# A fused attention and feed-forward kernel: the order of all pieces written out as one sequence in place of a list scheduler

## The chip, the cores and the metric

The kernel runs on one core of one Trainium2 chip. The metric is the device time of one execution in microseconds (us). Five engines work side by side, each through its own list of instructions in order: TensorE (PE, with its weight loads shown as PEld), VectorE (DVE), ScalarE (ACT), GpSimd (POOL) and SyncE (SP). POOL issues the loads; SP, and at the end ACT, issue transposing transfers and stores.

## The reference

Nyström attention over 8 batches, 8 heads, 576 rows of 64, with 32 landmark rows per head (means of 18 rows), and a feed-forward layer behind it. Everything is float32 in DRAM.

```python
q_lm = q.reshape(B, H, m, S // m, D).mean(axis=3)      # m = 32
k_lm = k.reshape(B, H, m, S // m, D).mean(axis=3)
A  = softmax(scale * q @ k_lm.T)                       # 576 x 32
Bm = softmax(scale * q_lm @ k_lm.T)                    # 32 x 32
C  = softmax(scale * q_lm @ k.T)                       # 32 x 576
Z = Bm.T / (norm_1(Bm) * norm_inf(Bm) + 1e-06)
for _ in range(6):
    Z = 2 * Z - Z @ Bm @ Z
x = (A @ Z @ C @ v)           # then heads side by side: 4608 x 512
h = x @ w_in                  # 512 x 2048
out = (h * sigmoid(h)) @ w_out # 2048 x 512
```

## The kernel before, in words

One pass over the 8 batches. The kernel first describes its work as 1,473 named pieces (`Op`, line 38), each with the engine or engines that may run it, the instructions that it emits, the pieces that it depends on, a priority, and the PSUM banks that it opens and releases. `Plan.run` (line 84) then puts all pieces into one order and gives each a PSUM bank, and the loop at line 1164 emits them in that order. What an engine executes is its own part of that order.

The pieces, by the names that the texts use (`.b` is the batch, `@5b00` and `@5b20` are the two row groups of batch b in layer 2, `@5340` and `@5740` a third group shared by four batches):

- `ld1`, `ld0` (lines 447, 453): loads of k (1) and q (0), for batch 0 in two halves each. `ldv0` to `ldv2` (460): three parts of v. `wi..` (467, 471): three loads for each quarter of `w_in`. `wo0` to `wo3` (477): quarters of `w_out`. All on POOL; at most eight are under way.
- `const` and `ident` (487 to 499): constants; `zer` feeds the filler products.
- `tr`, `trc` (568, 406/404): transposes of q and k on PE and copies out, for batches 0 to 2. From batch 3 on `xt10, xt11, xt00, xt01` (592), transposing transfers on SP, in their place. `ct0`, `ct1` (856) are the same for the exponentials of C from batch 2 on (`ctm`, `ctc` on PE and DVE or ACT before).
- `lms`, `lmc` (394, 404): landmark sums on PE for batches 0 and 1; `lra` to `lrd` (628): the same by additions on DVE from batch 2 on. `ltr`, `lmT`: their transposes.
- `sb`, `pb`, `pbs`, `pbr`, `bmx`, `bmt`, `csb`, `bbd`, `n1`, `nrm`: Bm with its softmax and norm; `pb` is an Exp on ACT.
- `f0`, `stz`, `stf`, and six times `ns` (PE) and `nsd` (DVE, line 754): the Newton iteration for Z. Each step waits for the one before.
- `A`, `Ax`, `S`, `Ln`, `Rs`, `etn`: the softmax of A; `C`, `Cx`, `wrc`: that of C. `A` and `C` open four banks at once and are 16 small products on parts of PE ("packed"). `Ax`, `Ln`, `Rs` and `Cx` are ACT's.
- `cv`, `wc`, `zbd`, `zt`, `ztc`: C @ v and Z times it. `m0` to `m3` and copies `mc` (404 on ACT, 406 on DVE): that times a quarter of `w_in`, so that layer 1 is `etn` times `m`.
- `h0` to `h15` and `hx0`, `hx8` (PE, 394): layer 1; `g..` and `gx..` (ACT, 956 and 979): Silu on the way out of PSUM. Silu and Exp/Ln are in different ACT tables, and each change between them is a table load.
- `o0` to `o3`, `oc`: layer 2 of the first group, plain. All other groups are done as pairs (`layer2_pair`, line 1025) with seven products `p1` to `p7` in place of eight, sums `ss` and `wt` on DVE beforehand, and `c..`, `u2` as evacuations into an output tile `ost` (a ring of six). `os..` stores it.

`Plan.run` of before is a list scheduler. It keeps a clock of its own, durations from simple formulas (lines 302 to 311), a lag after each piece, and a margin of 0.4 us in front of most PE pieces. Whenever an engine is idle in that clock it takes the ready piece of lowest priority number, to which the table `ORDER` (line 19) adds a correction for some fifty pieces. Other rules: no Silu between the Exp/Ln pieces of a batch, and PSUM pools: layer 2 gets banks 7, 6 and 5, layer 1 at most four of banks 4 to 0 (one, while a batch of Exp/Ln is pending), the rest the lowest free of 0 to 5 or 6. An evacuation that may run on ACT or DVE (`either`, line 413) goes to whichever is idle. While PE has nothing ready in the first 45 us of that clock, it gets a filler (`warm`, line 495): a product of zeros of 256 columns into bank 7.

Two waits are part of the description and not of the order: a transposing transfer of batch b waits for the second v load of batch b (line 594, `gate`), and the loads of batch b for the third transfer `xt00` of batch b-1 and for `ct0` of batch b-2 (line 1141).

Of the kernel before, what the change touches and what calls it, by code (L numbers as in the profile page):

```python
# [18 lines left out]
ORDER = {  # L19
    "f0.0": (200.69, 0), "A.0": (-135.46, 12.93), "Ln11.0": (-57.289, 0), "etn1.0": (-31.554, 0),  # L20
    "ctm00.0": (-1364.2, 0), "wc.0": (-5319.5, 0), "mc11.0": (-629.91, 0), "tr10.1": (-42.668, 0),
    "trc15.1": (-1007.6, 0), "tr19.1": (-457.92, 0), "tr114.1": (-85.703, 0),
    "tr00.1": (-4845.1, 0), "tr09.1": (-1.1208, 0), "tr014.1": (-139.96, 0),
    "lms116.1": (413.98, 0), "lms000.1": (-607.71, 0), "lms006.1": (-83.37, 0),
    "lms010.1": (328.48, 0), "nsd00.1": (-627.38, 0), "ns10.1": (2306.7, 0),
    "nsd10.1": (-1204.8, 0), "A.1": (-266.77, 0), "Ax10.1": (-230.29, 0), "Rs1.1": (-127.11, 0),
    "Cx00.1": (-281, 0), "Cx01.1": (-181.38, 0), "Cx11.1": (-2693.4, 0), "tr014.2": (-314.54, 0),
    "bbd.2": (-120.57, 0), "nsd40.2": (175.02, 0), "h15.1": (234.98, 0), "lrd1.3": (-791.6, 0),
    "A.3": (-480.16, 0), "S00.3": (52.867, 0), "Ln01.3": (24.258, 0), "Ax11.3": (-2.2697, 0),
    "h3.2": (185.78, 0), "hx0.2": (41.862, 0), "h11.2": (452.76, 0), "hx8.2": (-6.3754, 0),  # L30
    "p5@5200.0": (-179, 0), "c12@5220.0": (-251.23, 0), "A.4": (-78.982, 0),
    "etn1.4": (1667.8, 0), "Cx11.4": (29.753, 0), "cv0.4": (-3300.5, 0),
    "p6@5340.0": (-4.9303, 0), "p7@5340.0": (-4146.8, 0), "Ax10.6": (162.02, 0),
    "ss00@5500.0": (-5226.2, 0), "p7@5700.0": (633.04, 0), "p4@5720.0": (524.17, 0),
}
# [31 lines left out]
class Plan:  # L67
# [3 lines left out]
    WARM = 45.0  # L71
# [9 lines left out]
    start_warm = 1.1  # L81
    filler = None

    def run(self):
        import heapq
        order = []
        for o in self.ops:
            o.left = len(o.deps)
            shift, o.ready = ORDER.get(o.name, (0.0, 0.0))
            o.prio += shift  # L90
            for d in {id(d): d for d, _ in o.deps}.values():
                d.users.append(o)
        cand = {e: [] for e in self.LAG}
        idle = {"PE": 1.0, "ACT": 1.0, "DVE": 0.9, "POOL": 1.3, "SP": 1.0}
        banks = [0] * 8
        table = ["exp"]
        group = [None, 0]
        pending = [False]
        groups = {}
        for o in self.ops:  # L100
            if o.group is not None:
                groups[o.group] = groups.get(o.group, 0) + 1
        tiled = [None]
        dmaq = [0.0]
        events = sorted(set(idle.values()) | {o.ready for o in self.ops})
        waiting = []

        def activate(o):
            for e, _ in o.engs:
                cand[e].append(o)  # L110

        for o in self.ops:
            if not o.left:
                activate(o)

        l1_at = set()
        l1_open = {}
        l1_seen = set()
        l2_on = [False]
        l2_open = {}  # L120
        wide = [False]

        def fit(o):
            if o.cls == "L2":
                pool = (7, 6) if wide[0] else (7, 6, 5)
                if o.pair is not None and l2_open:
                    n = sum(not banks[i] for i in pool)
                    if o.pair != next(iter(l2_open)) and (o.pair in l2_open or n < 2):
                        return None
            elif o.cls == "L1":  # L130
                room = 1 if pending[0] or group[0] is not None and group[1] > 3 else 4
                if wide[0]:
                    return None
                if len(l1_at) >= room:
                    return None
                pool = (4, 3, 2, 1, 0)
            else:
                pool = (0, 1, 2, 3, 4, 5) if l2_on[0] else (0, 1, 2, 3, 4, 5, 6)
            free = [i for i in pool if not banks[i]]
            return tuple(free[:o.psum]) if len(free) >= o.psum else None  # L140

        n = 0
        total = len(self.ops)
        while n < total:
            if not events:
                raise RuntimeError("plan stuck: " + ", ".join(
                    f"{o.name}" for e in cand for o in cand[e])[:600])
            t = heapq.heappop(events)
            while events and events[0] <= t + 1e-9:
                heapq.heappop(events)  # L150
            moved = True
            while moved:
                moved = False
                for e in ("PE", "ACT", "DVE", "POOL", "SP"):
                    if idle[e] > t + 1e-9:
                        continue
                    best, bslot, later, soon = None, None, None, None
                    if e == "PE":
                        wide[0] = any(o.psum == 4 and o.ready <= t + 1e-9 and (
                            o.opens is None or group[0] == o.opens) for o in cand[e])  # L160
                    for o in cand[e]:
                        r = o.ready + o.margin
                        if r > t + 1e-9:
                            if later is None or r < later:
                                later = r
                            if o.crit and (soon is None or r < soon):
                                soon = r
                            continue
                        rank = o.prio
                        if e == "PE" and tiled[0] and o.tiled == tiled[0]:  # L170
                            rank -= 1e5
                        if best is not None and rank >= brank:
                            continue
                        if e == "ACT" and o.table == "silu" and group[0] is not None:
                            continue
                        if e == "ACT" and o.group is not None and group[0] != o.group:
                            if o.early is not None and table[0] == "exp":
                                pass
                            elif group[0] is not None or l1_open:
                                continue  # L180
                            elif o.early is not None and any(
                                    x.done is None or x.done > t + 1e-9 for x in o.early):
                                continue
                            elif len(l1_at) > 2:
                                pending[0] = True
                                continue
                        if o.opens is not None and group[0] != o.opens and (
                                group[0] is not None or l1_open or len(l1_at) > 2):
                            if group[0] is None and not l1_open:
                                pending[0] = True  # L190
                            continue
                        s = None
                        if o.psum:
                            s = fit(o)
                            if s is None:
                                continue
                        best, bslot, brank = o, s, rank
                    if best is None:
                        if later is not None:
                            heapq.heappush(events, later)  # L200
                        if e == "PE" and not banks[7] and self.start_warm <= t < self.WARM and (
                                later is None or later > t + 0.12):
                            end = t + (0.22 if t < self.start_warm + 4.4 else 0.11)
                            order.append((self.filler, e, t, end, False))
                            idle[e] = end
                            heapq.heappush(events, end)
                            tiled[0] = None
                        continue
                    o = best
                    if soon is not None and not o.crit:  # L210
                        d = max(d2 for e2, d2 in o.engs if e2 == e)
                        if t + d > soon + 0.06:
# [3 lines left out]
                    for e2, d2 in o.engs:  # L216
                        cand[e2].remove(o)
                        if e2 == e:
                            dur = d2
# [95 lines left out]
def kernel(  # L315
# [95 lines left out]
    A = P.add  # L411
# [794 lines left out]
```

## Time and profile before

| | us |
|---|---|
| median of three runs | 249.36 |
| the three runs | 247.73, 249.66, 249.36 |
| span of the profiled execution, first to last instruction | 246.7 |
| PE busy in it | 238.9 |
| ACT busy in it | 183.6 |
| DVE busy in it | 171.8 |
| share of the chain that ended last that is PE's | 83% |

The span of the profiled execution lies 1.0 to 3.0 us below the three runs' own times; the page gives no other time of that execution. In the lines of groups: source line, engine, operation, tile written and tiles read, count, busy time and mean duration of one in ns, then the idle time before them and what ended it. In a timeline: start, length (from the first start to the last end of a merged row), engine, line, operation, tiles and count. A matmul's record covers its way through the array, so that records of back-to-back matmuls overlap; the distance between starts is what each costs PE.

### The profile page before, as it was taken

Reading aid. Unit: us, or ns where it says so; the run is one execution under the profiler, and the core shown is the slowest. Engines: PE = TensorE matmul, PEld = TensorE weight load, DVE = VectorE, ACT = ScalarE, POOL = GpSimd, SP = SyncE. Lnnn points to the kernel's source line nnn. Section 1 sums busy time; section 2 is a strip of 40 time slices with the busy share of each in tenths; the row PEclk is TensorE's granted clock in tenths of the full one; section 3 lists DMA queues with packets and bytes.
Section 4 is the critical chain, followed back from the end, with each engine's and each line's share of the span. In section 5 each row is a group of like instructions: output and inputs, shape, how many; then the busy total and the mean of one; then the engine's idle time right before and its main releaser. Section 6 shows DMA issues by size and latency. Waiting matters only on the chain.

```text
span 246.7 us, 7075 instructions
## 1 busy us (share of the span) xinstructions
PE 238.9 (97%) x2771; PEld 170.8 (69%) x2771; DVE 171.8 (70%) x441; ACT 183.6 (74%) x438; POOL 37.2 (15%) x63
## 2 busy tenths in 40 slices
PE   8999999999979999999999999999999999999993
PEld 6786565566767645577886655697886566688883
DVE  2368956495869956949999879189798667066632
ACT  2597996599865999998668998966988978822200
POOL 8435733200022003200220040000000000000000
PEclk9999999999999999999999999999999999999999
DMA  5999999999999979989899799897443003022352
GB/s 103 203 203 193 196 208 206 207 246 166 181 115 215 208 145 152 212 135 158 168 233 229 150 170 226 146 184 99 118 119 101 0 3 85 3 73 62 82 141 72
DMA packets 55874, 36.50 MB, mean 148 GB/s; under 512 B 36641, under 2 KB 47393, under 8 KB 55841
## 3 DMA queue, kind: packets, MB, share of 16 engines
q0 software_dynamic: 15264, 18.35, 44.6%
q1 hardware_dynamic: 39808, 16.92, 33.2%
q10 hardware_dynamic: 768, 0.79, 1.3%
q8 instruction: 21, 0.34, 0.5%
q14 instruction: 13, 0.10, 0.1%
HBM read 36.70 MB, written 9.44 MB: 187 GB/s over the span
## 4 chain that ended last, share of the span: by engine, by line
PE 83%; DMA 7%; DVE 3%; ACT 3%; SPq 1%; issue 1%; POOL 0%; DVEq 0%; POOLq 0%
PE ps L394 80%; DMA qT<-qk 4%; DMA qk<-in_q_dram 3%; PE ps L568 2%; SPq L592 1%; ACT m L404 1%; DVE red L628 1%; PE ps L844 1%; DVE st L754 1%; ACT ce L829 1%; ACT L956 1%; POOL qk L447 0%; ACT ln L794 0%; DVE etn L803 0%; DVE ss L1044 0%
## 5 line engine op out<-in xcount | busy, mean ns | idle before, releaser
L394 PE MATMUL ps<-etn,m 128*128 128x512 bf16 (+1 forms) x512 | 68.9, 286 | 0.4 <-ACT gm L956 0.4
L956 ACT ACTIVATE gm<-ps 128x512 f16<-128x512 f32 x128 | 66.1, 652 | 2.0 <-PE ps L394 1.8
L394 PEld LDWEIGHTS <-gm 128*128 128x128 f16 x512 | 48.7, 98 | 11.3 <-issue 2.4
L394 PE MATMUL ps<-w_out_sb,gm 128*128 128x256 f16 (+1 forms) x392 | 53.6, 281 | 0.0
L394 PEld LDWEIGHTS <-m 128*128 128x128 bf16 x512 | 32.0, 98 | 24.0 <-issue 1.8
L404 ACT COPY ost<-ps 128x256 f32<-128x256 f32 (+1 forms) x48 | 18.4, 383 | 37.4 <-PE ps L394 30.3
L394 PEld LDWEIGHTS <-ss 128*128 128x128 f16 x408 | 39.1, 98 | 6.6 <-issue 0.9
L1079 DVE TENSOR_TENSOR ost<-ost,ps 128x256 f32<-128x256 f32 x51 | 21.2, 416 | 20.4 <-PE ps L394 14.2
L394 PE MATMUL ps<-wt,ss 128*128 128x256 f16 x272 | 34.1, 273 | 0.0
L754 DVE SCALAR_TENSOR_TENSOR st<-st,ps 128x320 bf16<-128x320 bf16 (+3 forms) x54 | 21.4, 404 | 9.0 <-PE ps L394 7.8
L406 DVE CAST m<-ps 128x512 bf16<-128x512 f32 x31 | 20.0, 683 | 0.4 <-PE ps L394 0.2
L406 DVE COPY ost<-ps 128x256 f32<-128x256 f32 x22 | 9.3, 422 | 14.9 <-PE ps L394 14.8
L404 ACT CAST m<-ps 128x512 bf16<-128x512 f32 x33 | 17.9, 601 | 1.8 <-PE ps L394 1.7
L394 PE MATMUL ps<-w_out_sb,ss 128*128 128x256 f16 x136 | 17.6, 273 | 0.0
L453 POOL DMA_DIRECT2D qk<-in_k_dram x7 | 5.0, 714 | 82.7 <-DMA ct<-ce 41.9
L460 POOL DMA_DIRECT2D v<-in_v_dram x24 | 14.0, 591 | 14.5 <-PE ps L394 6.9
L394 PE MATMUL ps<-zer 128*128 128x256 bf16 x79 | 14.7, 310 | 1.1 <-DVE zer L487 1.1
L394 PE MATMUL ps<-wt,gm 128*128 128x256 f16 x120 | 15.5, 272 | 0.0
L394 PEld LDWEIGHTS <-st 128*128 128x128 bf16 x96 | 8.4, 97 | 9.0 <-issue 2.9
L394 PE MATMUL ps<-st 128*128 128x160 bf16 (+1 forms) x96 | 14.4, 225 | 0.2 <-DVE wsb L889 0.2
L829 ACT ACTIVATE ce<-ps 128x288 bf16<-128x288 f32 x32 | 12.8, 413 | 0.0
L784 ACT ACTIVATE et<-ps 128x288 bf16<-128x288 f32 x32 | 10.6, 423 | 2.3 <-PE ps L394 2.2
(91 smaller groups left out, 331.3 us busy)
## 6 DMA issues: line engine op xcount, KB each, us to landing
out_dram<-ost SPq DMA_DIRECT2D x128, 64.0 KB, 2.1
v<-in_v_dram POOLq DMA_DIRECT2D x24, 192.0 KB, 11.2
qk<-in_k_dram POOLq DMA_DIRECT2D x7, 576.0 KB, 7.5
qk<-in_q_dram POOLq DMA_DIRECT2D x7, 576.0 KB, 10.6
w_out_sb<-in_moe_w_out_dram POOLq DMA_DIRECT2D x4, 512.0 KB, 10.4
w_in_sb<-in_moe_w_in_dram POOLq DMA_DIRECT2D x4, 256.0 KB, 9.2
w_in_sb<-in_moe_w_in_dram POOLq DMA_DIRECT2D x8, 128.0 KB, 7.9
qk<-in_k_dram POOLq DMA_DIRECT2D x2, 288.0 KB, 4.3
```

Source lines behind the costliest of these rows:

```text
L394: nc.tensor.matmul(out=out_ap, lhsT=lhsT, rhs=rhs, start=start, stop=stop, skip_group_check=True)
L404: nc.scalar.copy(out=out, in_=in_)
L406: nc.vector.tensor_copy(out=out, in_=in_)
L453: lambda e, t=t, src=src: nc.gpsimd.dma_start(out=qk_r[b % 2][:, t].rearrange("p g j d -> p g (j d)"), in_=src[b].rearrange("(g h) (l j) d ...
L460: lambda e, a=a: nc.gpsimd.dma_start(out=v_r[b % 2][a * L:(a + 1) * L, :, :], in_=v[b].rearrange("h (l a x) d -> a l h (x d)", l=L, a=VA)[ ...
L568: nc.tensor.transpose(out=ps[:, n * 128:(n + 1) * 128], in_=qk[:, t, g, 2 * jp:2 * jp + 2, :].rearrange("p j d -> p (j d)"), identity=idb)
L592: lambda e, t=t, g=g: nc.sync.dma_start_transpose(out=qT[:, t, g], in_=qk[:, t, g].rearrange("p j d -> p (j d)")),
L754: nc.vector.scalar_tensor_tensor(out=s2[:, g0:g1, lo:SW], in0=s[:, g0:g1, lo:SW], scalar=2.0, in1=ps[:, 0:NG * SW].rearrange("p (g x) -> p ...
L784: lambda e, g=g, et=et, c=c: nc.scalar.activation(out=et[:, c], in_=bank(me["A"], 2 * g + c)[:, 0:HS], func=AF.Exp, scale=sc / J),
L829: nc.scalar.activation(out=ce[:, :, 0:VP].rearrange("p (i c) (a l) -> p c a i l", c=2, a=VA)[:, c], in_=bank(me["C"], 2 * g + c)[:, 0:HS]. ...
L956: lambda e, dc=dc, cell=cell: nc.scalar.activation(out=gm[:, dc, :], in_=bank(cell["o"]), func=AF.Silu),
L1079: nc.vector.tensor_tensor(out=out_, in0=x, in1=y, op=OP.add)
```

## The change

`ORDER` and the scheduler go. In their place stands `SEQUENCE`, a text that names every piece once, in the order of emission, with the engine behind a slash where a piece may run on two, and `*n` for n fillers. `Plan.run` walks through it, checks that a piece comes after those that it depends on, and deals PSUM banks from one list: a piece takes the bank at its head, and a bank goes to its tail when the last piece that reads it has been placed in the sequence. Banks 0 to 6 are in the list from the start, bank 7 joins with the first piece of layer 2 (until then fillers write to it). The pools, the limit on layer 1's banks, the margin and the rule on Silu are gone with the scheduler.

PE's list has 53 fillers in place of 79: 22 instead of 20 ahead of the first load, and 31 instead of 59 later. All other products are the same. 77 evacuations change their engine (39 from ACT to DVE, 38 from DVE to ACT). ACT's table loads stay 12, its first included. Line numbers of pieces are 74 lower in the changed kernel, since the scheduler was longer than the sequence.

In `layer1` the product `hx` also names the copies of the first quarter that it reads among its dependencies.

The diff, cut to the new `run`, the parts of the sequence that the texts speak of, and `hx`:

```diff
-ORDER = {
-    "f0.0": (200.69, 0), "A.0": (-135.46, 12.93), "Ln11.0": (-57.289, 0), "etn1.0": (-31.554, 0),
...
-}
+SEQUENCE = """
+ld00.0 const ident *22 tr00.0 lms000.0 lms006.0 lms0012.0 ld01.0 *5 lms010.0 lms016.0 lms0112.0
+tr09.0 tr014.0 trc014.0/DVE tr05.0 trc05.0/ACT trc00.0/ACT ld10.0 *1 lms100.0 lms106.0 tr15.0
+trc15.0/ACT lmc0.0/DVE ltr0.0 lmT0.0/DVE trc09.0/DVE ld11.0 lms1012.0 *4 lms110.0 lms116.0
+lms1112.0 lmc1.0/ACT tr114.0 trc114.0/DVE tr10.0 trc10.0/ACT *1 ltr1.0 lmT1.0/DVE tr19.0
+trc19.0/DVE *3 A.0 Ax10.0 sb.0 pb.0 pbs.0 pbr.0 bmx.0 Ax00.0 Ax11.0 Ax01.0 *4 C.0 Cx00.0 Cx11.0
+Cx01.0 Cx10.0 bmt.0 S10.0 Ln10.0 *2 csb.0 n1.0 bbd.0 ld1.1 lms100.1 lms106.1 *2 f0.0 tr19.1
...
+ltr0.1 lmT0.1/ACT tr00.1 trc00.1/DVE trc15.1/ACT ctm00.0 ns30.0 nsd30.0 ctc00.0/DVE sb.1 pb.1 *1
+C.1 Cx11.1 Cx10.1 Cx00.1 pbs.1 pbr.1 bmx.1 Cx01.1 ns41.0 ns40.0 nsd40.0 nsd41.0 wi0a ldv0.0 ldv2.0
+ldv1.0 cv0.0 cv1.0 wc.0 ns50.0 nsd50.0 csb.1 *2 ns51.0 nsd51.0 n1.1 zbd.0 bmt.1 bbd.1 nrm.1 *3 A.1
+Ax11.1 zt.0 ztc.0/DVE Ax00.1 Ax10.1 Ax01.1 ctm00.1 S11.1 Ln11.1 f0.1 stz.1 stf0.1 ctc00.1/DVE
+wi0b1 wi1a wi0b0 m0.0 mc01.0/ACT mc00.0/ACT *2 ns00.1 S01.1 Ln01.1 nsd00.1 wi2b1 wi1b0 wi1b1 m1.0
+mc11.0/DVE mc10.0/DVE S10.1 Ln10.1 S00.1 Ln00.1 Rs1.1 ctm10.1 ns10.1 nsd10.1 h2.0 ctc10.1/DVE *1
+h7.0 wi2a wi2b0 m2.0 mc20.0/DVE mc21.0/DVE Rs0.1 g2.0 h4.0 ns20.1 nsd20.1 g7.0 h6.0 h0.0 g0.0 h5.0
+g6.0 wi3a wi3b0 wi3b1 m3.0 mc30.0/DVE mc31.0/DVE h10.0 g10.0 h1.0 g1.0 ns30.1 h9.0 nsd30.1 h3.0
...
+etn1.1 wo0 h15.0 o0@5001.0 h11.0 g11.0 ldv1.1 ldv0.1 ldv2.1 cv0.1 wrc.1 fold wc.1 g4.0 o0@5000.0
+zbd.1 g5.0 g15.0 zt.1 ztc.1/ACT h13.0 g13.0 wo1 o1@5001.0 etn0.1 m3.1 mc30.1/DVE m2.1 mc31.1/ACT
+mc21.1/ACT mc20.1/DVE m0.1 mc00.1/ACT mc01.1/DVE o1@5000.0 ld1.2 tr15.2 tr19.2 trc19.2/DVE
...
+trc05.2/ACT o2@5000.0 wo3 o3@5000.0 oc@5000.0/ACT g13.1 o3@5001.0 oc@5001.0/ACT lrb1.2 lrc1.2
...
+ss30@5100.0 sb.2 hx0.1 gx0.1 pb.2 pbs.2 ld1.3 ldv1.3 xt11.3 xt10.3 lra1.3 pbr.2 p5@5020.0
+c5@5020.0/ACT p6@5020.0 u2@5020.0/ACT p1@5100.0 c1@5100.0/ACT l1done.0 C.2 Cx10.2 Cx01.2 Cx00.2
+Cx11.2 ld0.3 xt00.3 p3@5020.0 c12@5020.0 bmx.2 lrb1.3 bmt.2 ss00@5120.0 lrc1.3 p6@5100.0
+u2@5100.0/ACT A.2 Ax11.2 Ax10.2 l1done.1 p7@5020.0 c22@5020.0 Ax00.2 Ax01.2 S11.2 Ln11.2 csb.2
+n1.2 S10.2 Ln10.2 p5@5100.0 c5@5100.0/ACT lrd1.3 ltr1.3 S01.2 lmT1.3/ACT bbd.2 S00.2 f0.2 Ln00.2
+Ln01.2 Rs1.2 Rs0.2 p4@5020.0 p7@5100.0 c21@5020.0/ACT xt01.3 lra0.3 nrm.2 lrb0.3 lrc0.3 stz.2
+lrd0.3 ltr0.3 stf0.2 etn1.2 c22@5100.0 p3@5100.0 etn0.2 lmT0.3/ACT sb.3 pb.3 ns00.2 nsd00.2
+p4@5100.0 c21@5100.0/ACT pbs.3 c12@5100.0 ns10.2 nsd10.2 ct0.2 ct1.2 A.3 Ax11.3 Ax00.3 Ax10.3
+Ax01.3 ss10@5120.0 ldv0.2 ldv1.2 ldv2.2 cv0.2 wrc.2 wc.2 C.3 Cx10.3 Cx00.3 ns20.2 pbr.3 p1@5120.0
...
+g9.2 g4.2 nsd30.3 ns40.3 nsd40.3 ldv1.4 ct0.3 ld0.4 ld1.4 ldv0.3 ct1.3 ldv2.3 cv0.3 xt00.4 ld1.5
...
+os11@5741.0/ACT os13@5741.0/ACT os12@5741.0/SP p3@5740.0 c12@5740.0 os13@5740.0/ACT os11@5740.0/SP
+os10@5740.0/SP os12@5740.0/ACT p4@5740.0 c21@5740.0/DVE os03@5741.0/ACT os00@5741.0/SP
+os01@5741.0/ACT l1done.6 l1done.7 os02@5741.0/SP
+"""
...
     def run(self):
...
+        named = {o.name: o for o in self.ops}
+        free = list(range(7))
+        table = "exp"
         order = []
...
+        seen = set()
+        for word in SEQUENCE.split():
+            if word[0] == "*":
+                order += [(self.filler, "PE", 0.0, 0.0, False)] * int(word[1:])
+                continue
+            name, _, e = word.partition("/")
+            o = named.pop(name)
+            assert all(id(d) in seen for d, _ in o.deps), name
+            seen.add(id(o))
+            if o.psum:
+                if o.cls == "L2" and 7 not in seen:
+                    seen.add(7)
+                    free.append(7)
+                assert len(free) >= o.psum, name
+                o.slot = tuple(free[:o.psum])
+                del free[:o.psum]
+            e = e or o.engs[0][0]
+            switch = e == "ACT" and o.table is not None and o.table != table
+            if switch:
+                table = o.table
+            order.append((o, e, 0.0, 0.0, switch))
+            for p, i in o.frees:
+                p.readers[i] -= 1
+                if not p.readers[i]:
+                    free.append(p.slot[i])
+        assert not named, sorted(named)
         return order
...
                 o = cell["o"] = A(f"hx{d0}.{b}", [("PE", mm_us(64, 16))], xm,
-                                  etn_ops[b] + m_ops[b, dc // 4]
+                                  etn_ops[b] + m_ops[b, d0 // 4] + m_ops[b, dc // 4]
                                   + l2_last.get(("x", b // 4 - 1), []), p + 0.5, psum=1, cls="L1")
```

## The prediction

> **What bounds the kernel now.** I read the page first: busy shares, slices, chain.
>
> ```profile
> span 246.7 us, 7075 instructions
> PE 238.9 (97%) x2771; PEld 170.8 (69%) x2771; DVE 171.8 (70%) x441; ACT 183.6 (74%) x438; POOL 37.2 (15%) x63
> ...
> PE   8999999999979999999999999999999999999993
> ...
> PEclk9999999999999999999999999999999999999999
> DMA  5999999999999979989899799897443003022352
> ...
> PE 83%; DMA 7%; DVE 3%; ACT 3%; SPq 1%; issue 1%; POOL 0%; DVEq 0%; POOLq 0%
> ```
>
> TensorE (PE) is busy from end to end and carries 83% of the chain; ACT and DVE have 63 and 75 us to spare. But busy PE hides two things: matmul records overlap, and fillers (the products of `zer`) count as busy. So I took the groups by shape, then the PE timeline at a few places.
>
> ```profile
> L394 PE MATMUL ps<-zer 128*128 128x256 bf16 x79 | 14.7, 310 | 1.1 <-DVE zer L487 1.1
> ```
>
> ```profile
> 1.12 4.43 PE L394 MATMUL ps<-zer 128*128 128x256 bf16 x20 [1.12 <-DVE zer L487]
> ...
> 12.33 0.20 PE L394 MATMUL ps<-lmT 64*32 64x32 bf16 x4
> ```
>
> ```profile
> 51.34 1.89 PE L394 MATMUL ps<-etn,m 128*128 128x512 bf16 x8
> ```
>
> ```profile
> 72.74 0.27 PE L394 MATMUL ps<-rs,fold 128*128 128x256 f16 x1 [1.63 <-DVE st L754]
> ```
>
> ```profile
> 88.64 0.59 PE L394 MATMUL ps<-etn,m 128*128 128x512 bf16 x2 [0.39 <-ACT gm L956]
> ...
> 96.43 0.62 PE L394 MATMUL ps<-w_in_sb,zt 64*32 64x512 bf16 x16
> ```
>
> ```profile
> 241.93 1.04 PE L394 MATMUL ps<-wt,gx 128*128 128x256 f16 x8
> ```
>
> Start to start, a matmul of 512 columns takes 0.216 us here, one of 256 0.109. The program's matmuls at that pace, fillers left out: 288 of 512 columns 62.2; 964 of 256 105.1; the 256 packed `w_in` products 8.0; the packed A and C 4.8; the `v` products 6.2; 400 of 64 columns 11.6; 184 of 128 10.3; 80 of 160 5.5; 32 of 288 3.9; the rest 1.9. Together 219.5 us. Both orders hold exactly these. So an order is judged by one quantity: clock time minus work done, "lost" below. The lines above are the starts of sb.0, h0.1, ltr1.3, (a wait of h5.2,) m0.3 and the last p4; counted through the order, the work before them is 4.3, 36.3, 55.5, 76.9 and 218.6 us, so 8.0 is lost at 12.33, 15.0 at 51.34, 17.2 at 72.74, 19.5 at 96.43, 23.3 at 241.93. Of those 23.3, 8.0 is waiting for q and k; 7.0 goes between 12 and 51 us; 2.2 up to 72.74, nearly all in one hole; 2.3 up to 96.43; and 3.8 in the last 145 us, about 0.1 at each switch to or from packed products, which any order pays. The end (last product's start to end of span, 4.8 us) is the same four products, evacuation and stores in both orders.
>
> The hole at 71 us is a transfer, by the chain in order of time, the timeline, and SP's own waits:
>
> ```profile
> 65.43 5.38 DMA qT<-qk
> ...
> 70.93 0.69 DVE red L628
> ```
>
> ```profile
> 70.93 0.69 DVE L628 TENSOR_TENSOR red<-qT 128x1024 f16<-128x1024 bf16 x1 [1.93 <-DMA qT<-qk]
> ```
>
> ```profile
> SPq L592 <- DMA v<-in_v_dram: 24.7, 3, 10.3
> ```
>
> Batch 3's transposes wait on SP for its second v load (landed 60.98), are issued 61.14 to 65.43, the last lands at 70.81, and DVE stands with batch 2's Newton step queued behind.
>
> **The change, part by part.**
>
> *Fillers.* 79 become 53: 22 instead of 20 at the front, 31 instead of 59 after. 28 x 0.109 = 3.05 us less inside. The two at the front end beside the first load (lands 5.17) and the second (6.69): 0.
>
> *First score.* q is loaded ahead of k, `ident` moves between POOL's first two loads (0.34 us of POOL). Landings in the trace (5.17, 6.69, 8.76, 10.19) are 1.4 to 2.1 apart, more than POOL's 0.55 per issue, so the shift hides under the first transfer; if not, it costs 0.34. Behind the fourth load stand the same steps in both orders (18 short products, lm copy, two products, lmT copy): A.0 at 12.3, 8.0 lost, as now.
>
> *12 to 51 us.* Now 7.0: 44 fillers x 0.109 = 4.8, waits 1.1, switches 1.1. The new order has 17 fillers there (1.85), the switches, and waits that I add up along queues, with issue times start to start (a Silu shows 652 ns, but eleven take 5.50 us from 88.00, 0.48 each). C.1 waits for pb.1 on ACT: 0.4. The longest is ACT behind A.1: four Ax (0.29 each), four Ln (1.16), two m copies (0.95), two Rs (1.15), the Silu table (1.28) and four Silu (0.477 each) = 7.6 us until g6.0 frees its bank for ns30.1; PE has 6.3 of work and 0.3 of fillers meanwhile; with 0.3 of handovers the wait is 1.3. Sum 1.85 + 1.1 + 1.7 = 4.65 against 7.0: **-2.3**. The loads bound it: m3.0 needs all of `w_in`, which lands at 30.27 and by the same bytes does so again; at 18.8 of work that is at least 11.5 lost. wo3 (q and k of batch 2 ahead of it) cannot land before 48.9, at 38.5 of work: 10.4. So the gain is at most 15.0 - 11.5 = 3.5; at least 0, if idle stands wherever a filler stood.
>
> *Batch 3's transposes.* On POOL, k.3 and v1.3 now go ahead of q.3, and all of v.2 behind: v1.3 lands at 56.00 (k.3 now) - 3.5 (three v.2) + 1.0 = about 53.5 instead of 60.98, and the first two transposes stand first on SP. Their issue (1.4 each) and 3.3 to 5.0 us to landing give 57 to 60. DVE needs them at about 59.8. Hole gone: **-2.0** (0 to -2.2). Late next is v.2, by about 60, needed by cv0.2 at 56.2 of work + 12.9 lost by then (8.0 + 4.65, and switches) = 69: covered by 9 us.
>
> *76 to 96 us.* The wait of h.2 for a bank (0.39 on the page, a table load and few banks for layer 1) has no counterpart: banks 0 to 6 are dealt first-freed-first. **-0.6** (0 to -1.0).
>
> *SP's later stores.* os@5000.0 now follows ct1.2 (issued by 64; four store issues and 2.1 to landing: 69); c1@5120 needs the buffer at 58.3 of work, about 71. os@5020.0 stands behind two of batch 5's transposes, which wait for v1.5 and so for cv0.3 (near 85), and is through by 94; its buffer is needed at 103. Hidden, 2 and 9 us of cover; without, PE waits by the shortfall.
>
> *ACT to DVE and back* (38 and 39 copies change sides). By the rows (m copy 0.477 on ACT, 0.601 on DVE; ost copy 0.269, 0.341), ACT's issue time goes from 168 to 167 us, DVE's from 161 to 161. Neither becomes the bound: 0. *`hx` dependency*: its m copies end earlier on their queues anyway: 0. *After 96 us* I added up the ACT or DVE queue between every product and what it releases and found no place where it is longer than the PE work between; switches stay 3.8: 0 (-0.7 to +2, an unseen wait or two of the 1.3 size).
>
> Sum: -2.3 - 2.0 - 0.6 = -4.9, so a span near 241.8. The median of before is 2.7 above the profiled span; 249.36 - 4.9 = 244.5.
>
> **Two rules against the rows.** The first 20 fillers start 0.21 us apart (4.43 us in all), later ones 0.109, under a granted clock of 1.00: PE begins at half pace. The Trainium skill ("TensorE: Matmul & The Clock Gate", Part 1) says PE falls back to that pace after an idle window of about 3.4 us, which speaks against taking fillers out. By it one fallback for such a window would add an estimated 1.7 us, 246.2; no wait that I add up here is over 1.3 us.
>
> The transposes of 61 to 65 us took 3.3, 3.5, 3.4 and 5.4 us to land with the loads nearly over; now loads of q.3 and v.2 run beside them. The skill ("DMA: Bandwidth & Descriptors", Queues, rings and completion order) says each DMA engine takes turns between queues packet by packet. If that doubled the slowest, an estimate, the second would land near 66 and the sum be some 3.5 us more, 248.
>
> **Rivals.**
>
> *A, forecast, 244.5.* Chance 0.72, own range 242 to 246.8.
>
> *B, the gain is mostly eaten.* Idle stands where fillers stood (for: ACT is 27.3 of 31 us busy from 9 to 40; against: the sum of 1.3) and later waits cost 0.7: 249.36 - 2.6 + 0.7 = 247.5. Chance 0.15.
>
> *C, slower: DVE is blocked by the transposes.* lra1.3, the reader of both k transposes, now stands right behind pbs.2, so the whole Newton chain of batch 2 queues behind a DMA. PE has work until csb.2 (50.4 + 12.9 = 63.3), which follows lra1.3 by about 1.2 us of DVE: a landing later than 62.1 is paid one for one. At 70.8, where the last lands now, it is 8.7 us: 253.2. It breaks even at a landing of 67 and shows as slower from 69.5. For: 5.4 us once, and loads beside it; against: issue is 7.5 us earlier. Chance 0.11, with other mishaps of its size 0.13.
>
> *D, nothing changes:* excluded; PE's list is 26 fillers shorter and differs almost from its first product.
>
> **How the numbers follow.** A measurement of this kernel tells about 1% (2.5 us) from no change: before alone spans 247.73 to 249.66. Faster than 246.9 is A, 0.72; within is B, 0.15; slower is C, 0.13. Low end: 249.36 - 3.5 - 2.2 - 1.0 - 0.7 = 242.0. Up to 250.5 takes in B and the mild part of C; what is left out above is about 0.1, below 0.07.
>
> **What would show it.** Right: 53 `zer` matmuls; work 36.3 us reached near 49 instead of 51.3; the first transposes issued near 54; no DVE wait for qT of over 0.5 us; PE from 96 us on losing some 4 us as now. Wrong: PE waits over 0.5 us behind DVE red or ACT gm; landings of k.3's transposes past 62; a granted clock under 1; waits after 96 us adding up to more than 2.

## The result and the profile after

| | before | changed |
|---|---|---|
| median, us | 248.97 (four runs) | 260.31 (four runs) |
| runs, us | 247.73, 249.66, 249.36, 248.58 | 256.32, 258.27, 262.67, 262.36 |
| span of the profiled execution, us | 246.7 | 254.6 |
| ratio to before, 95% interval | | 1.0337 (1.0257 to 1.0417) |

The changed kernel is slower by 2.6 to 4.2%. The forecast was 244.5, the range ended at 250.5. The ratio leaves out the changed kernel's two slowest runs, 262.67 and 262.36, whose granted clock was lower (0.974 and 0.979, in the others 0.992 and 0.985). The profiled execution of the changed kernel is the fastest of its four, so the text accounts for the 7.9 us between the profiled spans, not for the 11.3 between the medians. Its page:

```profile
span 254.6 us, 7003 instructions
PE 238.6 (94%) x2745; PEld 168.9 (66%) x2745; DVE 174.5 (69%) x442; ACT 182.7 (72%) x437; POOL 37.3 (15%) x63
...
PE   8599999999799999299999999979999999999994
...
PEclk9999999999999999979999999999999999999999
DMA  5999999999839999977889999984521152002354
...
PE 69%; DMA 14%; ACT 7%; DVE 6%; issue 1%; SPq 1%; POOL 0%; DVEq 0%; POOLq 0%; ACTq 0%
```

PE's row, 9 almost throughout before, has a 2 in the slice that begins at 101.8 us, and the clock's row a 7 in the next one. DMA's share of the chain has doubled, from 7 to 14%, but half of the 14 are stores (`out_dram<-ost`), and the transposes' share (`qT<-qk`) is 4% in both. The chain passes the hole by a store that landed at 106.92; DVE did not wait there, it was busy with lra1.4 to lrd1.4 until 106.91. So the waits below tell more than the chain. PE's timeline in the changed kernel, at the first score, at a wait for a copy on ACT, at ltr1.3, around the 2, and at the last `p4`:

```profile
14.34 0.44 PE L320 MATMUL ps<-qT,lmT 64*32 64x288 bf16 x16
...
62.94 1.03 PE L320 MATMUL ps<-w_out_sb,ss 128*128 128x256 f16 x8 [0.42 <-ACT ost L330]
...
68.93 0.28 PE L320 MATMUL ps<-rs,fold 128*128 128x256 f16 x1 [0.75 <-DVE rs L554]
...
106.97 0.28 PE L320 MATMUL ps<-rs,fold 128*128 128x256 f16 x1 [4.75 <-DVE rs L554]
...
108.99 1.91 PE L320 MATMUL ps<-etn,m 128*128 128x512 bf16 x4
...
249.93 1.04 PE L320 MATMUL ps<-wt,gx 128*128 128x256 f16 x8
```

The measure "lost" of the prediction (clock time less work done) makes the two orders comparable at equal work. The table gives it for the profiled execution of each kernel, counted from the starts of the products; the kernels after the first two are the experiments below.

| work done, us | 4.4 | 36.3 | 60 | 79 | 90 | 110 | 150 | 218 (end) |
|---|---|---|---|---|---|---|---|---|
| before | 8.0 | 15.1 | 18.1 | 19.9 | 19.9 | 20.6 | 22.1 | 23.3 |
| changed | 10.1 | 14.9 | 17.8 | 18.5 | 25.6 | 26.8 | 30.0 | 31.3 |
| a1_ident_last | 8.0 | 13.3 | 15.3 | 16.1 | 23.9 | 25.0 | 30.8 | 32.2 |
| a2_gate5 | 9.5 | 15.1 | 16.6 | 17.9 | 17.9 | 24.5 | 30.3 | 31.7 |
| a3_loads | 9.8 | 14.6 | 15.9 | 16.7 | 16.7 | 22.3 | 28.1 | 29.5 |
| a4_both | 7.9 | 12.8 | 15.1 | 15.8 | 15.9 | 21.8 | 27.7 | 29.1 |
| a5_dve | 7.9 | 12.8 | 15.2 | 16.0 | 16.0 | 22.7 | 25.8 | 27.1 |
| a7_stores | 7.7 | 12.8 | 15.2 | 16.0 | 16.0 | 19.5 | 22.6 | 23.9 |
| b1_ident_second | 9.5 | 16.8 | 17.8 | 21.2 | 21.3 | 21.9 | 23.4 | 24.7 |
| b2_gate5 | 8.2 | 16.1 | 17.1 | 32.4 | 32.4 | 33.1 | 34.6 | 35.8 |
| b3_deal | 8.1 | 15.5 | 17.3 | 18.4 | 18.4 | 19.1 | 20.4 | 21.5 |

The 8.0 us of the changed kernel are therefore: +2.1 up to the first score, -2.3 to 36.3 of work, -0.1 to 60, -1.1 to 79, and +9.4 behind that, 7.1 of these between 79 and 90. At 79 of work the changed kernel is still 1.4 us ahead.

What happens there is on DVE and on the queues. The changed kernel's waits, DVE's timeline and POOL's and SP's, then POOL's and SP's lines for the same loads and transposes before:

```profile
DVE red L554 <- DMA qT<-qk: 14.4, 4, 8.8
```

```profile
105.11 0.69 DVE L554 TENSOR_TENSOR red<-qT 128x1024 f16<-128x1024 bf16 x1 [8.80 <-DMA qT<-qk]
```

```profile
90.70 0.71 POOL L379 DMA_DIRECT2D qk<-in_k_dram  x1 [12.54 <-DMA qT<-qk]
91.40 1.17 POOL L386 DMA_DIRECT2D v<-in_v_dram  x2
...
```

```profile
83.30 10.24 SPq L518 DMA_TRANSPOSE qT<-qk  x4
```

```profile
96.83 0.71 POOL L453 DMA_DIRECT2D qk<-in_k_dram  x1 [19.98 <-DMA qT<-qk]
```

```profile
88.98 6.53 SPq L592 DMA_TRANSPOSE qT<-qk  x4
```

The time from issue to landing of all twenty transposes, before and in the changed kernel:

```profile
DMA to landing us min/median/max: 3.2/3.4/5.4
```

```profile
DMA to landing us min/median/max: 3.2/4.6/13.9
```

lra1.4 on DVE waits 8.80 us for xt11.4, the last of the four transposes of batch 4. The trace has its issue at 91.11 and its landing at 105.02: 13.9 us, where all twenty transposes of before took 3.2 to 5.4. POOL's next six loads, four of batch 5 and two of v of batch 4, are issued from 90.70 and land from 97.27 to 106.74: the transpose runs beside them. Before, the loads of batch 5 were issued from 96.83 on, when all four transposes of batch 4 had been issued and three had landed. The wait that keeps the two apart names pieces by their description: transposes wait for a batch's second v load, and the next batch's loads for xt00. In the scheduler's order the first was the next to last load and the second the third of four transposes. In the sequence ldv1.4 is the first load of its batch and xt00.4 the first transpose. Both waits are still there, but the loads now wait for one transpose of four, and the other three can run beside them.

### The profile page after: what moved, and what is told of

Read it like the earlier page. It is cut to its first block, busy times and chain, and to the rows that moved or that the text cites. A ratio compares the mean times of both kernels' runs of the same rounds, so it can differ in the third digit from the quotient of the medians.

```text
span 254.6 us, 7003 instructions
## 1 busy us (share of the span) xinstructions
PE 238.6 (94%) x2745; PEld 168.9 (66%) x2745; DVE 174.5 (69%) x442; ACT 182.7 (72%) x437; POOL 37.3 (15%) x63
## 4 chain that ended last, share of the span: by engine, by line
PE 69%; DMA 14%; ACT 7%; DVE 6%; issue 1%; SPq 1%; POOL 0%; DVEq 0%; POOLq 0%; ACTq 0%
PE ps L320 67%; DMA out_dram<-ost 7%; DMA qT<-qk 4%; DMA qk<-in_q_dram 3%; ACT gm L882 2%; PE ps L494 2%; DVE ss L970 1%; SPq L947 1%; DVE red L554 1%; ACT ost L330 1%; ACT pb L619 1%; ACT qT L330 1%; DVE gm L970 1%; ACT L1085 1%; ACT lmT L330 0%
## 5 line engine op out<-in xcount | busy, mean ns | idle before, releaser
L882 ACT ACTIVATE gm<-ps 128x512 f16<-128x512 f32 x128 | 69.5, 644 | 6.6 <-PE ps L320 6.2
L320 PE MATMUL ps<-etn,m 128*128 128x64 bf16 (+1 forms) x512 | 71.9, 288 | 0.3 <-DVE lmT L332 0.2
L320 PE MATMUL ps<-w_out_sb,gm 128*128 128x256 f16 (+1 forms) x392 | 54.5, 283 | 0.0
L330 ACT COPY ost<-ps 128x256 f32<-128x256 f32 (+1 forms) x47 | 18.0, 401 | 17.8 <-PE ps L320 17.3
L1005 DVE TENSOR_TENSOR ost<-ost,ps 128x256 f32<-128x256 f32 x51 | 20.9, 415 | 12.3 <-PE ps L320 9.9
L330 ACT CAST m<-ps 128x512 bf16<-128x512 f32 x33 | 17.9, 598 | 1.1 <-PE ps L320 1.1
L554 DVE TENSOR_TENSOR red<-qT 128x1024 f16<-128x1024 bf16 x12 | 8.3, 690 | 15.1 <-DMA qT<-qk 14.4
L970 DVE TENSOR_TENSOR ss<-gm 128x1024 f16<-128x1024 f16 x15 | 10.3, 684 | 8.7 <-ACT gm L882 8.7
L320 PE MATMUL ps<-wt,gm 128*128 128x256 f16 x120 | 15.5, 273 | 0.1
L720 ACT ACTIVATE ln<-ps 128x288 f32<-128x288 f32 x32 | 12.4, 427 | 3.6 <-PE ps L320 3.5
L755 ACT ACTIVATE ce<-ps 128x288 bf16<-128x288 f32 x32 | 12.9, 427 | 2.1 <-PE ps L320 2.0
```

The costliest lines, as they stand in the source:

```text
L320: nc.tensor.matmul(out=out_ap, lhsT=lhsT, rhs=rhs, start=start, stop=stop, skip_group_check=True)
L330: nc.scalar.copy(out=out, in_=in_)
L554: lambda e: nc.vector.tensor_tensor(out=o_, in0=a_, in1=b_, op=OP.add),
L720: lambda e, g=g, c=c, ln=ln: nc.scalar.activation(out=ln[:, c], in_=bank(me["S", g, c])[:, 0:HS], func=AF.Ln),
L755: nc.scalar.activation(out=ce[:, :, 0:VP].rearrange("p (i c) (a l) -> p c a i l", c=2, a=VA)[:, c], in_=bank(me["C"], 2 * g + c)[:, 0:HS]. ...
L882: lambda e, dc=dc, cell=cell: nc.scalar.activation(out=gm[:, dc, :], in_=bank(cell["o"]), func=AF.Silu),
```

## The experiments

Theory 1: ident between POOL's first two loads holds the second back. Theory 2: loads beside transposes stretch the transposes, DVE stands at their reader, and PE behind it. Against both stands the rival that the written order of PE, ACT and DVE or the banks dealt in turn are slow by themselves. Experiments a1 to a8 start from the changed kernel, b1 to b4 from the kernel before.

**a1_ident_last and b1_ident_second: ident.**

```diff
-ld00.0 const ident *22 tr00.0 lms000.0 lms006.0 lms0012.0 ld01.0 *5 lms010.0 lms016.0 lms0112.0
...
+ld00.0 ld01.0 ld10.0 ld11.0 const ident *22 tr00.0 lms000.0 lms006.0 lms0012.0 *5 lms010.0
...
```

> The changed kernel with one step undone: ident goes behind the four first loads on POOL instead of between the first and the second; the order of the loads stays. Theory 1 (ident between two loads holds back the second): the second load lands near 6.7 instead of 9.47, the fourth near 10.2 instead of 12.28, A.0 starts near 12.3 instead of 14.3, and the time falls by 2.0 to 2.5 us. Rival (the second load is late because q goes first, or the late data were no bound): landings within 0.5 us of the changed kernel's or a gain below 0.7 us.

```diff
     order = P.run()
+    named = {r[0].name: r for r in order}
+    order.remove(named["ident"])
+    order.insert(order.index(named["ld10.0"]) + 1, named["ident"])
```

> The kernel before with one step of the change alone: ident is put between POOL's first and second load. Theory 1: the second load lands near 9.5 instead of 6.69, A.0 or sb.0 starts some 2 us later than before, and the time rises by 1.5 to 2.3 us. Rival (q first, not ident): landings as before and a time within 0.5 us.

The landings came as theory 1 said: the second load at 6.64 in a1 (9.47 in the changed kernel, issued 0.34 later), at 8.87 in b1 (6.69 before, issued 0.36 later); A.0 in a1 starts at 12.3. In the summary of POOL's first four loads, the changed kernel and a1:

```profile
L373 POOL DMA_DIRECT2D qk<-in_q_dram x2: 575/630/686, 1.3 to 2.3; - x2
...
DMA to landing us min/median/max: 3.9/7.6/8.8
```

```profile
L373 POOL DMA_DIRECT2D qk<-in_q_dram x2: 549/618/686, 1.3 to 2.0; - x2
...
DMA to landing us min/median/max: 3.9/5.2/6.9
```

The time did not follow in a1. It measured 257.26 (254.14 to 260.61), 1.0294 times before (1.0206 to 1.0382), which overlaps the changed kernel's interval: 2.5 us are still held at 60 of work, then the hole at ltr1.4 is 5.60 us in place of 4.91, and another of 2.74 opens at 152. PE came to ltr1.4 2.5 us earlier (its last product ahead of the hole starts at 99.37, in the changed kernel at 101.84), and xt11.4 landed only 1.8 earlier (103.23). In b1 it did follow: 249.70, ratio 1.0062 (1.0032 to 1.0091), 1.4 us more lost at the end. Theory 1 is right on the lateness. What that costs is 0.8 to 2.3 us in b1, by the ratio's interval, and nothing that can be told in a1, where a transfer ends the next stage.

**b4_memset: what of ident it is.**

```diff
+    spare = constp.tile([128, 128], BF, tag="spare", name="spare")
+    order.insert(order.index(named["ld10.0"]) + 1, (Op(
+        "spare", [("POOL", 0.1)], lambda e: nc.gpsimd.memset(spare, 0.0)), "POOL", 0.0, 0.0, False))
```

> The kernel before with a POOL memset of 128x128 into a spare tile between POOL's first and second load; ident stays behind the fourth. It tells what of ident holds the second load. If any POOL operation between two loads does it: the second load lands near 8.9, as with ident there, in place of 6.6. If it is ident's own operation, with what the program loads for it: the second load lands within 0.4 us of 6.6, and the time is within 1 us of before.

The second load landed at 7.63, between the two; the time was 249.17, ratio 1.0035 (0.9996 to 1.0074). A memset of 0.2 us on POOL made the load 0.9 us later, ident (0.3 us) 2.2 to 2.8; 0.14 and some 0.35 of that is the later issue. What the rest of ident's delay comes from stays open.

**a2_gate5 and b2_gate5: one wait.** a2 moves the wait of batch 5's loads to the third transpose that is issued; no engine's list changes. b2 takes the same wait out of the kernel before.

```diff
-... cv0.3 xt00.4 ld1.5 xt01.4 ldv1.5 ldv2.4 ld0.5 ns50.3 ... g15.3 xt10.4 mc00.3/DVE
+... cv0.3 xt00.4 xt01.4 ns50.3 ... g15.3 xt10.4 ld1.5 ldv1.5 ldv2.4 ld0.5 mc00.3/DVE
...
-        gate = last[b - 1].get("xts", [])[-2:-1]
+        gate = last[b - 1].get("xts", [])[:1] if b == 5 else last[b - 1].get("xts", [])[-2:-1]
```

> The changed kernel with one semaphore moved: batch 5's loads wait for xt10.4, the third transpose that SP issues, instead of xt00.4, which the sequence puts first; every engine's list stays. Theory 2 (the loads of batch 5 beside batch 4's transposes stretch these tenfold): xt11.4 lands near 95 instead of 105.02, ltr1.4 starts near 102 instead of 106.97 without a wait of PE, the granted clock from 100 to 120 us is 0.99 or more instead of 0.91, and the time falls by 6.5 to 8 us, to a span of 246.5 to 248. Rival (the written order itself, or SP's own lateness, holds DVE): xt11.4 still lands past 100, or another wait takes the place, and the time falls by less than 3 us.

```diff
+    named = {r[0].name: r[0] for r in order}
+    for n in ("ld1.5", "ld0.5", "ldv0.5", "ldv1.5", "ldv2.5"):
+        named[n].after = [x for x in named[n].after if x is not named["xt00.4"]]
```

> The kernel before with one wait taken from batch 5's five loads: they no longer wait for the third transpose of batch 4, only for ct0.3 as before, and so run beside all four. Theory 2: the transposes of batch 4 land 6 to 14 us after their issue instead of 3.3 to 5.0, DVE's lra1.4 or lra0.4 waits for them, PE stands at ltr1.4 or ltr0.4 for 3 to 9 us, and the time rises by 3 to 9 us. Rival (a transpose takes its 3 to 5 us whatever runs beside it): landings below 6 us after issue and a time within 1 us.

b2 is the clearest of all runs: 260.59 us, ratio 1.0497 (1.0452 to 1.0543), from one wait less. Its transposes of batch 4 landed 8.8, 15.6, 11.0 and 5.6 us after their issue. PE and DVE in b2:

```profile
93.88 1.49 PE L394 MATMUL ps<-etn,m 128*128 128x64 bf16 x20
107.49 1.05 PE L394 MATMUL ps<-w_in_sb,zt 64*32 64x512 bf16 x16 [12.12 <-DVE zt L406]
```

```profile
106.40 0.69 DVE L628 TENSOR_TENSOR red<-qT 128x1024 f16<-128x1024 bf16 x1 [13.41 <-DMA qT<-qk]
107.01 0.42 DVE L406 CAST zt<-ps 128x256 bf16<-128x256 f32 x1
```

PE does not wait for the transposes' own data but for a copy of zt that stands behind lra1.4 on DVE. The rise is 12, more than the 3 to 9 expected, because I had priced the wait at ltr1.4 and not at that copy.

In a2, xt11.4 landed at 94.75, ltr1.4 started at 101.39, and the hole is gone: 17.9 lost at 90 of work, as at 79. But the time fell only to 255.18 (ratio 1.0284, 1.0236 to 1.0331); the span of the profiled execution was 255.0 where 246.5 to 248 was expected, a miss by 7 us. Another hole, of 4.14 us, opened 8 us after the old one's start, and with it came a new stretch at half clock, so that the mean clock between 100 and 120 stayed at 0.91; and one of 3.2 follows at 165.73. PE, then SP, in a2:

```profile
101.39 0.27 PE L320 MATMUL ps<-rs,fold 128*128 128x256 f16 x1
...
109.29 0.65 PE L320 MATMUL ps<-qT,lmT 64*32 64x288 bf16 x16
113.80 1.44 PE L320 MATMUL ps<-wt,ss 128*128 128x256 f16 x6 [3.87 <-ACT ost L330]
```

```profile
102.89 6.27 SPq L518 DMA_TRANSPOSE qT<-qk  x2
109.26 1.92 SPq L947 DMA_DIRECT2D out_dram<-ost  x4
```

The loads of batch 5 start 4 us later now, and its own transposes, with whatever stands behind them on SP, are the next thing that is late.

**a3_loads and a4_both: POOL's list put back from batch 4 on, without and with a1's edit.**

```diff
-... ldv1.4 ct0.3 ld0.4 ld1.4 ldv0.3 ct1.3 ldv2.3 cv0.3 xt00.4 ld1.5 xt01.4 ldv1.5 ldv2.4 ld0.5 ...
+... ld1.4 ld0.4 ldv0.3 ldv2.3 ldv1.4 ldv0.4 ldv2.4 ct0.3 ct1.3 cv0.3 xt10.4 xt11.4 xt00.4 xt01.4
+ld1.5 ld0.5 ldv0.5 ldv1.5 ldv2.5 ...
-... xt01.5 xt00.5 ... ct0.4 ld1.6 ... cv0.4 ldv1.6 ld0.6 ... ct0.5 xt00.6 ld1.7 cv0.5 ldv1.7 ...
+... xt00.5 xt01.5 ... ct0.4 ld1.6 ld0.6 ... cv0.4 ldv0.6 ldv1.6 ldv2.6 ... ct0.5 xt10.6 xt11.6
+xt00.6 ld1.7 ld0.7 xt01.6 cv0.5 ldv0.7 ldv1.7 ldv2.7 ...
```

> The changed kernel with POOL's list from batch 4 on put back so that no load runs beside a transpose of q or k of batches 5 to 7, and hardly any of batch 4: k and q of a batch first, then v, its second v load next to last, and two pairs of transposes swapped so that xt00, for which the next batch's loads wait, is the third that SP issues. The lists of PE, ACT and DVE, the banks and ident stay as in the changed kernel. Theory 2: transposes of batches 5 to 7 land within 6 us of issue, no wait of PE over 1 us after 75 us, and the lost time at the end is 10.0 (first score) + 4.9 (to 51 us) + 2.5 (batch 3, left as it is) + 1.1 + about 4 = 22.5 us in place of 31.3: a span near 246, some 8.5 below the changed kernel's 254.6. Rival (the written order and the banks dealt in turn lose time by themselves): waits stay or move to ACT and DVE, and the span stays above 251.

> The changed kernel with POOL's list from batch 4 on put back as in a3_loads, and ident behind the four first loads as in a1_ident_last. Theories 1 and 2 together: 2 us less than a3_loads, a span near 244, and so faster than the kernel before by 1 to 2%. Rival (an earlier start only meets a later transfer, as in a1_ident_last, where 2 us won at the start were given back at 100 and 152 us): a span within 0.7 us of a3_loads.

a3: 255.38, ratio 1.0278 (1.0225 to 1.0331), span 252.8 in place of 246. a4: 254.03, ratio 1.0199 (1.0128 to 1.0270, which leaves open whether it is slower by 2%), span 252.4. The transposes of batch 5 landed 3.3 us after their issue in both, so theory 2's part came out, and at 90 of work a4 has lost 15.9 where before has lost 19.9. But both lose 5 to 6 us between 90 and 110 of work and 6 between 110 and 150. Half of the rival is right: with the transposes no longer stretched, the written order waits at other places. a4's 2 us at the start are again mostly gone at the end (0.4 of span).

**b3_deal: the banks alone.** The order of before, with PSUM banks dealt over it by the changed kernel's rule.

```diff
+    free, l2, left = list(range(7)), False, {}
...
+            o.slot = tuple(free[:o.psum])
+            del free[:o.psum]
...
+            if not left[id(p), i]:
+                free.append(p.slot[i])
```

> The kernel before with one part of the change alone: its order stays, and only the PSUM banks are dealt anew over it, from one list by the changed kernel's rule. Theories 1 and 2 put all of the loss on transfers: a time within 1 us of before. Rival (banks dealt in turn make PE wait for slow evacuations): the time rises by 2 us or more, with PE waiting for ACT or DVE at products that open a bank.

246.66 us, ratio 0.9926 (0.9905 to 0.9948): not the cause, but a gain of 0.5 to 1.0%, and the one kernel here that is faster than both. Of its 1.8 us, 1.2 come at the hole of 71 us and 0.6 at the wait of h5.2. b3's PE beside the prediction's line at 72.74:

```profile
71.31 0.27 PE L394 MATMUL ps<-rs,fold 128*128 128x256 f16 x1
72.03 0.31 PE L394 MATMUL ps<-st 128*128 128x160 bf16 x2 [0.45 <-DVE st L754]
```

ltr1.3 no longer waits. Before, the plan had given it the bank of ns00.2, which nsd00.2 (line 754, the releaser that the old line names) had still to read, and nsd00.2 stood on DVE behind lra0.3 and its transfer. The hole that I had put down to the transfer needed the bank as well; with another bank two thirds of it go.

**a5_dve and a6_dve_only: theory 3, the readers' places on DVE.**

```diff
-... ss20@5200.0 lra1.5 lrb1.5 ss30@5200.0 lrc1.5 ... lrd1.5 ... csb.4 lra0.5 ... lrb0.5 f0.4 stz.4 stf0.4 lrc0.5 ...
+... ss20@5200.0 ss30@5200.0 ... csb.4 ... f0.4 stz.4 stf0.4 lra1.5 lrb1.5 lrc1.5 lrd1.5 ... c22@5200.0 lra0.5 lrb0.5 ...
```

> a4_both with the readers of the transposes moved back on DVE: lra1.3 to lrd1.3 behind n1.2, lra1.5 to lrd1.5 behind stf0.4, lra0.5 and lrb0.5 behind c22@5200, lra1.7 to lrd1.7 behind n1.6, lra0.7 to lrd0.7 behind stf0.6, with their ltr and lmT, and xt01.7 ahead of one group of stores on SP. Theory 3 (what a4_both still loses, 5.4 us at 107 to 116 us and 4.7 at 161 to 170, is DVE standing at a reader that the sequence puts ahead of the transfer, with small steps of the Newton chain and the sums ss queued behind): both stretches lose less than 1 us each, batch 3's less than 1 in place of 2.0, the lost time at the end is 18 to 20.5 us in place of 29.1, a span of 241.5 to 244 and a time some 2% below the kernel before. Rival (the written order holds further waits of the kind): the span stays above 248.

> The changed kernel with the readers moved back on DVE as in a5_dve, but with its own order of loads and ident's place. If the readers' place alone was the cause (rival), the span falls to 247 or below. If both are needed (theories 2 and 3): xt11.4 still lands past 103 with a wait of PE of 4 us or more near 102, and only the holes of batches 3 and 7 shrink, by 2 to 3.5 us together: a span of 251 to 253.

a5: 252.88, ratio 1.0170 (1.0133 to 1.0207), span 250.4; batch 7's loss (110 to 150 of work) fell from 5.9 to 3.1, batch 5's did not (5.9 became 6.7 between 90 and 110), nor did batch 3's. Theory 3 holds for batch 7 and fails for batch 5. a6: 261.00, ratio 1.0470 (1.0416 to 1.0524): the hole at ltr1.4 is there (4.16), so the readers' places alone cure nothing; the holes of batches 3 and 7 did not shrink as expected, and one of 3.23 opened at 155.

**a7_stores: theory 4.** In a5 the wait between 107 and 110 us reads so, on ACT:

```profile
109.53 0.65 ACT L330 COPY ost<-ps 128x256 f32<-128x256 f32 x2 [1.82 <-DMA out_dram<-ost]
```

```diff
-... os@5021.0 p3@5220.0 xt10.5 xt11.5 sb.4 pb.4 p1@5200.0 os@5020.0 c1@5200.0/ACT ... os@5121.0 os@5120.0 ...
+... os@5021.0 p3@5220.0 os@5020.0 os@5121.0 os@5120.0 xt10.5 xt11.5 sb.4 pb.4 p1@5200.0 c1@5200.0/ACT ...
```

> a5_dve with one change on SP alone: three groups of stores (os@5020, os@5121, os@5120), whose data have long been done, go ahead of xt10.5 instead of behind it. In a5_dve xt10.5 waits for a load until 103.40, the stores behind it land past 108, and ACT's copy into their output tile starts at 109.53 after a wait of 1.82 us. Theory 4 (stores queued behind a waiting transpose hold the ring of output tiles): that wait and DVE's of 1.34 us for a store are gone, the 4.8 us lost between 107 and 119 us shrink to about 2, and the span falls from 250.4 to 247 to 248.5. Rival (DVE, crowded by the readers, is the bound there): the waits for stores go, but the span falls by less than 1 us.

249.26 us, ratio 1.0045 (1.0027 to 1.0063), span 247.2: 3.2 less than a5, as theory 4 said. SP and ACT in a7:

```profile
95.03 11.18 SPq L947 DMA_DIRECT2D out_dram<-ost  x14
106.37 5.58 SPq L518 DMA_TRANSPOSE qT<-qk  x4
```

```profile
107.72 0.65 ACT L330 COPY ost<-ps 128x256 f32<-128x256 f32 x2
```

The same copy on ACT starts 1.8 us earlier, without a wait. The transposes are issued 3 us later than in a5; that costs PE 0.5 us at ltr0.5.

**a8_rest: the remaining waits.** The readers moved once more; the diff shows batch 3's.

```diff
-... n1.2 lra1.3 lrb1.3 lrc1.3 lrd1.3 S10.2 Ln10.2 ... bbd.2 S00.2 f0.2 ...
+... n1.2 S10.2 Ln10.2 ... bbd.2 S00.2 f0.2 lra1.3 lrb1.3 lrc1.3 lrd1.3 ...
...
```

> a7_stores with the readers' places mended where a5_dve put them badly: lra1.3 to lrd1.3 behind f0.2 instead of ahead of bbd.2 (1.34 us of PE's wait for bbd), and ltr0.7, lmT0.7 and sb.7 some 1 to 2 us later on PE (1.81 us of PE's wait for rs). Theory 3: 2 to 3 us less than a7_stores, a span of 244 to 246, and a time some 1 to 1.5% below the kernel before. Rival (these waits only move to the next reader): within 0.7 us of a7_stores.

249.35, ratio 1.0060 (1.0035 to 1.0085), span 247.7. The rival was right: bbd's wait of 1.33 went and one of 1.21 at ltr0.3 came; 1.81 at ltr0.7 became 0.93 and 1.10.

## Why the prediction was wrong, point by point

The forecast was 4.9 us less lost than before; by the table the changed kernel loses 8.0 more. Of the 12.9 between the two 9.4 are the term "after 96 us", 2.1 the first score and 1.9 batch 3; 0.5 went the other way.

- **After 96 us, "0 (-0.7 to +2)": the step that failed.** I added up ACT's and DVE's queues behind every product, but the sum names no landing for xt.4, xt.5 and xt.7, though their readers stand in DVE's queue in front of what I added up. From 79 of work to the end the changed kernel loses 12.8 us against 3.4 before. Of the 9.4, a2 and b2 show 7.1 as one wait between loads and transposes: 4.9 at ltr1.4, 1.8 up to 110.85 with matmuls at half pace, and 0.4 at 112.00. Of the other 2.3, 1.45 is one wait at 169.88, for a sum on DVE behind the reader of batch 7's transposes, the kind that a5 mends; the rest was not followed up.
- **First score, "8.0 lost as now; if not, 0.34": wrong by 2.** I compared the gaps between landings with POOL's issue times, and took a POOL operation for no more than its length. a1 and b1 show the second load's data 2.2 to 2.8 us later with ident in front of it.
- **12 to 51 us, -2.3: right in size, in part by luck.** From 4.4 to 36.3 of work the changed kernel loses 4.8, forecast 4.65; before lost 7.1. The 17 fillers are 1.85 of it, as forecast. But the wait of 1.3 at ns30.1 is not there: no product in this part starts more than 0.43 us late, and the rest, forecast as 1.1 of switches and 1.7 of waits, is many small losses that add up to about the same.
- **Batch 3's transposes, -2.0: wrong.** v1.3 landed at 56.04, not 53.5, and the two k transposes, issued at 56.13 and 57.51 beside the loads of q.3 and v.2, took 8.6 and 8.1 us, not 3.3 to 5.0. The part lost 2.9 against 3.0. And b3 shows that 1.2 of the hole went with the banks alone.
- **76 to 96 us, -0.6: right in its cause, short in size.** b3, by the banks alone, has no wait at h5.2. The changed kernel loses 0.7 between 60 and 79 of work against 1.8, a gain of 1.1, just past the stated end of 1.0.
- **SP's later stores, 0 with 9 us of cover: the cover was counted in an order without the other waits.** In the changed kernel os@5020, forecast through by 94, is issued at 111.26; ACT's copy at 117.33 does not wait there. In a2 and a5 os@5020 behind xt10.5 holds ACT for 3.8 and 1.8 us.
- **Fillers:** 53 `zer` matmuls, and no stretch of 20 us up to 100 at a lower clock. **The copies that change sides, 0: nearly.** PE waits 0.42 us at 62.94 for c5@5020, now on ACT behind a table load and the four `pb`, and 0.22 at 112.00 for lmT1.4, now on DVE.
- **The two rules, both taken as an aside.** Between 100.00 and 102.00 us of the changed kernel the trace has 82 packets per us in the loads' queue, of 2,304 bytes, and 80 in the transposes', of 256 bytes. In b2 from 106.00 to 107.00, with the loads over, the transposes alone make 1,080 of 256 bytes. That is what the Trainium skill says ("DMA: Bandwidth & Descriptors", Queues, rings and completion order): each engine takes turns between queues packet by packet. With ninefold packets in the other queue, a transpose gets a tenth of the bytes. I used a doubling, on batch 3 alone. There it came out (the second transpose landed at 65.63, estimated 66); in batch 4 it is far too little.
- The page on the clock ("TensorE: Matmul & The Clock Gate", Part 1) has PE fall back after an idle window of some 3.4 us. In the trace, the clock granted after the hole of 4.91 is one half from 107.36 to 110.77, which makes the mean of the window below 0.91. Matmuls of 512 columns start 0.43 us apart from 108.99 to 110.70. The price up to 110.85 is 1.8 us, 0.3 of it a wait at ltr0.4, against the 1.7 estimated. Shorter waits did it too: PE's waits of 2.15 us in a5 (to 109.95), 2.74 in a1 and 2.76 in a4 were each followed by 3.4 us at half clock, one of 2.42 in a3 was not. So an idle window of 3.4 us is not needed; what else decides is open.

```profile
100.00:120.00 20.00, 14.87 (x127) 9.70 (x123) 13.60 (x32) 12.83 (x34) 0.00 (x0) 0.91 0.91 182
```

- **Rival C had the mechanism** (DVE blocked at lra1 behind transposes beside loads) at 0.11, one batch too early: in batch 3 PE lost about as much as before, in batch 4 the 7.1. That its 253.2 is the forecast nearest to the measured time is luck: it put the loss into batch 3.

The prediction's own signs of error came true: waits of PE over 0.5 us behind DVE's `red` and `rs`, landings of k.3's transposes at 64.74 and 65.63, a clock under 1, and waits after 96 us of more than 2 in all.

Open: why the runs of the changed kernel spread over 6 us where those of before spread over 2 (3.4 us at half clock take 0.007 off a run's mean clock, so by an estimate from that the clocks of 0.992, 0.985, 0.979 and 0.974 stand for one to four such stretches; only the first run has a trace); the rest of ident's delay; and whether the written order, mended at all its waits, would beat b3_deal. At 90 of work a7_stores is 2.4 us ahead of b3_deal, at the end 2.4 behind.

## What to carry to other kernels

A wait that names a piece protects by that piece's place in a queue: after a reordering, look up each such wait and what now stands on either side of it. Price a transfer by what runs beside it at that moment, and follow its reader's engine: what waits is what stands behind the reader, often something else than its data. When an early stage is sped up and the time stays, look where the next transfer ends; here each wait taken away (loads, readers, stores) showed the one behind it, and the end moved by less than the wait (in a2 the 7.1 were gone, and the time fell by about 2).

## What was not expected of the hardware

- A transposing transfer that takes 3.2 to 5.4 us in the kernel before took 8.8, 15.6, 11.0 and 5.6 beside plain loads in b2, and 13.9 in the changed kernel. The loads are slowed far less: in b2, k.5 landed 8.8 us after its issue and q.5 11.3, before 6.4 and 9.9.
- A POOL operation of 0.2 to 0.3 us between the first two loads delays the second one's data by 0.9 (memset, b4) to 2.8 us (ident).
- A wait of 12.1 us of PE in b2 brought the mean granted clock of the 20 us from 100 on to 0.74; in the changed kernel 4.9 us brought 0.91. In both, half clock went on for some 3.4 to 3.8 us after PE had work again.
